# Shifted token mixing with eleven packed matmuls a block instead of twelve

## The chip, the cores and the metric

The kernel runs on one core of a Trainium2 chip. The metric is device time in microseconds; the time before is the median of three runs. TensorE does the matmuls, VectorE, ScalarE and GpSimd the arithmetic on rows, and SyncE issues the DMAs.

## The reference, cut to what matters

```python
xn  = _layernorm(x)                               # x: 2048 tokens x 448
out = x + irfft2(rfft2(xn) * W) + B(xn)

def B(x, w1, w2, w3, w4):
    h = _gelu(_layernorm(x) @ w1)                 # 448 x 448
    c = 112
    g0 = h[:, 0*c:1*c] shifted by +1 token        # zero at the ends
    g1 = h[:, 1*c:2*c] shifted by -1
    g2 = h[:, 2*c:3*c] shifted by +2
    g3 = h[:, 3*c:   ] shifted by -2
    x1 = x + concat(g0, g1, g2, g3) @ w2          # 448 x 448
    return x1 + _gelu(_layernorm(x1) @ w3) @ w4   # F = 1792
```

The change touches the line with `w2`: each output token takes four quarters of 112 channels from the tokens one and two before and after it.

## The kernel before, in words

**Tokens.** Token a*16 + b stands on partition a (0 to 127) in block b (0 to 15). A shift by one or two tokens is therefore a change of block, and at blocks 14, 15, 0 and 1 also a shift by one partition. The blocks are worked in four groups, `GRP` = 14, 15, 0, 1; then 2 to 5, 6 to 9, 10 to 13.

**Precision.** Each fp32 matrix product is done as three fp16 products: every operand is split in a high fp16 half and a fp16 remainder ("lo"), and hi x hi, hi x lo and lo x hi are summed in PSUM. `PASS` names these three.

**The stage in order.** 28 matmuls on zeros (`warm_up`) run while the first rows load. Normalised rows are transposed on TensorE (`T1`, for the first three groups) or by DMA (`turn`, for the last). `w1_in` makes the w1 product of a block, 11 matmuls: since 448 = 3 x 128 + 64, the two cross terms that have 64 rows share one matmul. `w1_unit` then applies the gelu in PSUM (ScalarE, L433), writes the hi half in fp16 (ScalarE, L434) and the lo half (VectorE, L435, one operation over 448 columns) into a buffer `hs_buf` of 2 x 4 quarters, each padded from 112 to 128 columns, and one DMA on SyncE's queue transposes that buffer (L438) into `hT[g]`, 8 tiles of 128 tokens. Group 0 has 16 zero columns ahead of each block, so that the shift over the partition edge is a slice that starts one column earlier or later.

`w2_tile(b)` (L442) then takes its four quarters from the transposed blocks b-1, b+1, b-2 and b+2, three passes each: 12 matmuls with 112 rows (L454). VectorE adds the result to the residual row (L456). `w2` arrives in one DMA on 112 partitions and is split into hi (ScalarE) and lo (GpSimd) in `w2p`.

Then comes `ln2`: the second layernorm, whose rows are split and transposed by DMA into `x2mem` (L490), and the channel MLP: `mlp_in` with w3 (L385), gelu, and the w4 product (L787). The Fourier part runs in the second half of the span beside the MLP.

**Memory.** `x2mem` holds, at different times, two of the five `hs_buf`, the raw w4 (four loads, L228) and the transposed `y` of the MLP. `w3raw` is loaded in parts; the last one (its t = 3) waits in the queue until the transposition of block 5 was issued.

**Order.** Engines run in program order as a scheduler has laid it out, by priority (`prio`) and by `behind(key)`, which keeps an operation behind others named in `after`. SyncE issues its DMAs in order too: one that waits holds up all that come later. In the stage its order before is: eight h transpositions as the units end, the w3raw rest, one h, four xT, two h between two y, the four w4 loads, two y, four h, `csm`.

Of the kernel before, what the change touches and what calls it, by code (L numbers as in the profile page):

```python
# [20 lines left out]
NB, NC = 16, 16  # L21
# [3 lines left out]
PASS = ((0, 0), (0, 1), (1, 0))  # L25
SHIFT = [1, -1, 2, -2]
WARM = 28
# [8 lines left out]
WMAX = [(1, 4), (1, 5), (1, 6), (2, 0), (2, 1), (2, 2), (2, 3), (2, 4)]  # L36
HS = 3
EVAC, FILL = 0, 100000
# [30 lines left out]
def constants():  # L69
# [20 lines left out]
    for c in range(NC):  # L90
        for j8, (k1, t) in enumerate(slots(c)):
            for j, (kr, s, base) in enumerate(rows(c)):
                if base != k1:
                    continue
                phi = tau * np.outer(np.arange(NB), kr + 128 * np.arange(16)) / S
# [28 lines left out]
def body(tc, nc, x, wf, w1, w2, w3, w4, c_g, c_n, c_small, out):  # L124
# [69 lines left out]
    def load_x(g):  # L194
        for b0 in sorted(GRP[g])[::2]:
            SY.dma_start(xt[b0 // 2], xv[:, b0:b0 + 2])

# [22 lines left out]
    load_w3([2])  # L220
    x2mem = pw.tile([128, 9 * F], F16, name="x2mem")
    x2all = x2mem[:, 0:8 * F].rearrange("p (j t n) -> p j t n", j=4, t=7)
    w4raw = x2mem.bitcast(F32)[:, F:].rearrange("p (f n) -> p f n", f=14)
    w4v = w4.rearrange("(f p) n -> p f n", p=128)
    W4F = (0, 4, 8, 11, 14)

    def load_w4(i):
        SY.dma_start(w4raw[:, W4F[i]:W4F[i + 1]], w4v[:, W4F[i]:W4F[i + 1]])  # L228

# [168 lines left out]
    def h_alloc(g):  # L398
        t = {0: 0, 1: 1, 2: 2, 3: 1}[g]
        hT[g] = pr.tile([128, 8, 512 if g else 592], F16, tag=f"h{t}", name=f"h{g}")  # L400
        if g == 0:
            P.memset(hT[g][:, :, 0:576].rearrange("p t (b a) -> p t b a", b=4)[:, :, :, 0:16], 0.0)
            P.memset(hT[g][:, :, 576:592], 0.0)

    def h_at(g, i):
        return 128 * i if g else 144 * i + 16

# [8 lines left out]

    hs_buf = [p1.tile([128, 2, 4, 128], F16, name=f"hs{i}") for i in range(HS)]
    for t in hs_buf:
        P.memset(t.rearrange("p i k n -> p (i k) n")[:, :, 112:], 0.0)

    for o in (0, 1024):
        hs_buf.append(x2mem[:, o:o + 1024].rearrange("p (i k n) -> p i k n", i=2, k=4))
        P.memset(hs_buf[-1].rearrange("p i k n -> p (i k) n")[:, :, 112:], 0.0)

    def w1_unit(g, i, pm=None):
        if pm is None:
            pm = bank(("tr" if g == 1 else "mm", "acc")[i // 2], f"pw1_{g}{i}")
            w1_in(g, [(i, pm)], range(4))
        c = CS[GRP[g][i]]
        pm = pm[:, :D]  # L430
        pv_ = pm.rearrange("p (k n) -> p k n", k=4)
        h = hs_buf[c % (HS if g == 3 else HS + 2)]
        A.activation(out=pm, in_=pm, func=AF.Gelu_apprx_tanh, scale=gsc[:, c:c + 1])  # L433
        u = A.activation(out=h[:, 0, :, 0:112], in_=pv_, func=AF.Copy, scale=h1)  # L434
        v = V.scalar_tensor_tensor(out=h[:, 1, :, 0:112], in0=pv_, scalar=h1, in1=h[:, 0, :, 0:112],  # L435
                                   op0=ALU.mult, op1=ALU.subtract)
        o = h_at(g, i)
        d = SY.dma_start_transpose(out=hT[g][:, :, o:o + 128], in_=h.rearrange("p i k n -> p (i k n)"))  # L438
        after[g, i] = u.ins, v.ins
        after["h", g, i] = (d.ins,)  # L440

    def w2_tile(b):  # L442
        pm = bank("sp", f"pw2_{b}")
        n = 0
        for k in (2, 0, 1, 3):
            src, o = b - SHIFT[k], 1
            if src < 0:
                src, o = src + NB, 0
            elif src >= NB:
                src, o = src - NB, 2  # L450
            g, i = WHERE[src]
            o += h_at(g, i) - 1
            for hi, wi in ((0, 0), (0, 1), (1, 0)):
                T.matmul(pm[:, :D], hT[g][:112, 4 * hi + k, o:o + 128], w2p[:, wi, k], start=n == 0, stop=n == 11)  # L454
                n += 1
        V.scalar_tensor_tensor(out=xb(b), in0=xb(b), scalar=cs[:, CS[b]:CS[b] + 1], in1=pm[:, :D],  # L456
                               op0=ALU.mult, op1=ALU.add)

    def ln2(bs, engines):
# [22 lines left out]
        for i in range(n):  # L482
            b, h, x_ = b0 + i, y[i // 2][:, i % 2], o[i // 2][:, i % 2]
            k = r[:, i:i + 1]
            u = A.activation(out=h[:, 0:D], in_=x_, func=AF.Copy, scale=k)
            V.scalar_tensor_tensor(out=h[:, 448:512], in0=x_[:, 384:448], scalar=k, in1=h[:, 384:448],
                                   op0=ALU.mult, op1=ALU.subtract)
            v = V.scalar_tensor_tensor(out=h[:, 512:896], in0=x_[:, 0:384], scalar=k, in1=h[:, 0:384],
                                       op0=ALU.mult, op1=ALU.subtract)
            d = SY.dma_start_transpose(out=x2all[:, b // 4][:, :, 128 * (b % 4):128 * (b % 4) + 128], in_=h)  # L490
            after[f"b{b0}"] = u.ins, v.ins, d.ins

    def unscale(p, part):
        t = part.rearrange("p (b n) -> p b n", b=2)
        SY.dma_start(t, xv[:, 2 * p:2 * p + 2])
        return lambda: V.scalar_tensor_tensor(out=xt[p], in0=xt[p], scalar=p12, in1=t, op0=ALU.mult, op1=ALU.add)

    def finish(b):
        t = xb(b)
        if b < 2:  # L500
            t = row()[:, :D]
            SY.dma_start(t, xv[:, b])
            V.scalar_tensor_tensor(out=t, in0=xb(b), scalar=p12, in1=t, op0=ALU.mult, op1=ALU.add)
        SY.dma_start(ov[:, b], t)

# [5 lines left out]
    def do_fold(b0):  # L511
        X = pfd.tile([128, 2, D + 1], F32, tag="xf", bufs=3, name=f"xf{b0}")
        after["X", b0] = (SY.dma_start(X[:, :, 0:D], xv[:, b0:b0 + 2]).ins,)
        with behind("f", *FOLD[b0 // 2]):
# [180 lines left out]
    def front(G, fp, tag):  # L695
        tok = slice(256 * (G % 2), 256 * (G % 2) + 256)
        pm = bank(tag, f"pw3_{G}{fp}")
        for ff in range(2):
            f = 2 * fp + ff
            mlp_in(pm[:, 256 * ff:256 * ff + 256], w3p, slice(128 * f, 128 * f + 128), x2all[:, G // 2], tok)  # L700
        with prio(EVAC):
# [65 lines left out]
    def back(G, fp):  # L767
# [10 lines left out]
        for i in range(2):  # L778
# [12 lines left out]
            if end:  # L791
                with prio(EVAC):
                    for r, to in parts:
                        V.scalar_tensor_tensor(out=xb(b)[:, r], in0=to, scalar=p34[:, min(G, 1):min(G, 1) + 1],  # L794
                                               in1=xb(b)[:, r], op0=ALU.mult, op1=ALU.add)
                        if G > 4:
                            SY.dma_start(ov[:, b, r], xb(b)[:, r])

# [50 lines left out]
    def w4_split(f):  # L849
        split_w(w4p[0][:, 0, f:f + 2], w4p[0][:, 1, f:f + 2], w4raw[:, f:f + 2], s4)  # L850

# [4 lines left out]
    with behind("n", 0):  # L856
        s1, r1 = powers(m1, 4, "1", "mm")
    h_alloc(0)
    first = [bank("mm" if k < 2 else "sp", f"pw1_0{k}") for k in range(4)]
# [12 lines left out]
    with behind("w1", 3):  # L872
        squares(m2[:112], flat(w2s[:112]))
    T1(1, range(3))
# [13 lines left out]
    with behind("a1"), behind("n", 2):  # L888
        for k in range(1, 4):
            w1_unit(0, k, first[k])  # L890
    with behind("na", 2):
        for k in range(4):
            split_w(w2p[:, 0, k], w2p[:, 1, k], w2s[:112, k], s2[:112], P)
    h_alloc(1)
    for k in range(4):
# [7 lines left out]
    with behind("a2"):  # L903
        n1 = [norm1(3, [P, P, P, P])]
    h_alloc(2)
    for k in range(4):
# [16 lines left out]
    for b in range(4, 8):  # L923
        w2_tile(b)
        with behind(*PIN[b - 4]):
            w3_split(2 * b - 8)
            w3_split(2 * b - 7)
            for i in (2 * b - 10, 2 * b - 9):
                if i >= 0:
                    squares(m4[:, i:i + 1], flat(w4raw[:, 2 * i:2 * i + 2]), junk4)  # L930
    squares(m4[:, 6:7], flat(w4raw[:, 12:14]), junk4)
    ln2([2, 3], [A, P])
    h_alloc(3)
    for k in range(4):
# [10 lines left out]
    for j in range(4):  # L945
        homes[j] = x2mem[:, F * j:F * j + F]
    w4t.update({j: m.rearrange("p (i k n) -> p i k n", i=2, k=4) for j, m in homes.items()})
# [121 lines left out]
```

## Time and profile before

| | |
|---|---|
| median of 3 runs | 410.78 us (410.74 to 410.94) |
| the profiled execution | 410.65 us |
| its span in the trace | 408.9 us |
| outside the span | 1.75 us |
| granted TensorE clock, mean | 1.0 |
| TensorE, VectorE, ScalarE, GpSimd busy | 98%, 81%, 63%, 23% of the span |
| the token-mixing product (L454) | 192 matmuls, 39.9 us, at 32.0 to 101.4 us |

A row of a timeline reads: start, length (us), engine, line, operation, output and input by their names in the program, tile sizes, count, and in brackets the idle time just ahead with what ended it. A group's row has count, busy time, mean of one in ns (matmuls overlap, so the mean is longer than the pitch), and idle time ahead. A row of the DMA view gives queue and operation, count, KB each, and the median time from issue to landing. In a DMA view of a window, the first row is the busy share of the 16 engines in 40 slices (9 is 90% or more), GB/s what was moved in each, and "packets" are the pieces.

### The profile page before, as it was taken

The page shows a single profiled execution, that of the slowest core. Times are in us where ns is not written, and L with a number is a line of the kernel's source. Part 1 is how long each engine was busy: PE and PEld are TensorE (multiplying, and loading weights), DVE is VectorE, ACT ScalarE, POOL GpSimd, SP SyncE. Part 2 cuts the span into 40 slices and gives each one's busy share as a digit, 9 for nine tenths or more (in the row PEclk, how much of TensorE's full clock was granted, in tenths as well). Part 3 has the DMA queues.
Part 4 walks back from the last instruction along what each step waited for, and adds up shares of the span by engine and source line. Part 5 has one row for each costly group of instructions (what it writes and reads, how often), then busy time and mean ns, then how long its engine had stood idle before and what let it go on. Part 6 is the DMA issues. An engine that isn't in the chain of part 4 may idle for free.

```text
span 408.9 us, 8745 instructions
## 1 busy us (share of the span) xinstructions
PE 402.3 (98%) x3409; PEld 299.0 (73%) x3409; DVE 330.7 (81%) x686; ACT 256.5 (63%) x434; POOL 95.3 (23%) x172
## 2 busy tenths in 40 slices
PE   7999999999999999999999999999999999999996
PEld 3655555765668777777887887877777779998995
DVE  4888999898857678887798888955899989966645
ACT  4698879973758866556598888863453554453431
POOL 3877720101336748400012111110000000000000
PEclk9999999999999999999999999999999999999999
DMA  8959879914786456516255666500011022100101
GB/s 278 354 192 179 153 149 321 177 62 90 156 231 202 137 196 210 170 59 183 63 145 143 155 156 171 147 27 3 24 68 69 25 88 85 55 2 2 45 2 45
DMA packets 56168, 51.28 MB, mean 125 GB/s; under 512 B 37632, under 2 KB 50496, under 8 KB 56128
## 3 DMA queue, kind: packets, MB, share of 16 engines
q1 hardware_dynamic: 56128, 50.74, 46.0%
q8 instruction: 26, 0.43, 0.4%
q14 instruction: 14, 0.11, 0.1%
HBM read 38.28 MB, written 3.67 MB: 103 GB/s over the span
## 4 chain that ended last, share of the span: by engine, by line
PE 94%; DVE 3%; DMA 2%; POOL 0%; issue 0%; ACT 0%; SPq 0%; POOLq 0%
PE pw L385 33%; PE acc L787 23%; PE pw L454 9%; PE pw L414 6%; PE side L757 4%; PE acc L757 3%; PE pu L646 3%; PE ps L543 3%; PE pe L667 2%; PE pp L601 2%; PE px L618 2%; PE py L688 2%; DVE sta L293 1%; DMA xt<-x 1%; DMA h<-hs 1%; PE pta L374 1%
## 5 line engine op out<-in xcount | busy, mean ns | idle before, releaser
L385 PE MATMUL pw<-x2mem,w3p 128*128 128x256 f16 x1232 | 151.1, 273 | 0.0
L385 PEld LDWEIGHTS <-w3p 128*128 128x128 f16 x1232 | 119.2, 98 | 20.6
L787 PE MATMUL acc<-w4p,hf 128*128 128x448 f16 (+1 forms) x516 | 105.4, 348 | 0.0
L787 PEld LDWEIGHTS <-hf 128*128 128x128 f16 x516 | 49.8, 98 | 36.5
L705 ACT ACTIVATE pw<-pw,pe 128x512 f32<-128x512 f32 x42 | 27.5, 655 | 35.7 <-PE pw L385 35.7
L708 DVE SCALAR_TENSOR_TENSOR hf<-pw,h,hf 128x512 f16<-128x512 f32 x42 | 31.3, 748 | 14.5 <-ACT hf L707 14.4
L454 PE MATMUL pw<-w2p,h 112*128 112x448 f16 x192 | 39.9, 352 | 0.8 <-DMA h<-hs 0.8
L414 PE MATMUL pw<-w1p,xT 128*128 128x448 f16 x176 | 35.4, 352 | 0.0
L627 POOL TENSOR_TENSOR z<-te 128x450 f32<-128x450 f32 x16 | 15.7, 982 | 70.3 <-DVE te L625 70.3
L454 PEld LDWEIGHTS <-h 112*128 112x128 f16 x192 | 18.6, 98 | 17.2 <-DMA h<-hs 1.0
L707 ACT ACTIVATE hf<-pw,h 128x512 f16<-128x512 f32 x42 | 28.7, 686 | 1.0
L414 PEld LDWEIGHTS <-xT 128*128 128x128 f16 x176 | 16.9, 98 | 16.4 <-DVE xT L379 0.8
L723 ACT ACTIVATE hz<-g,h 128x896 f16<-128x896 f32 x14 | 14.6, 1044 | 22.3 <-DVE g L720 22.2
L757 PEld LDWEIGHTS <-hz 128*128 128x128 f16 x294 | 28.2, 98 | 0.4
L608 ACT ACTIVATE pf<-pp 64x450 f16<-64x450 f32 x32 | 17.4, 544 | 12.3 <-DVE pf L609 8.0
L609 DVE TENSOR_TENSOR pf<-pp,pf 64x450 f16<-64x450 f32 x32 | 19.9, 622 | 3.4 <-ACT pf L608 3.0
L724 DVE SCALAR_TENSOR_TENSOR hz<-g,h,hz 128x896 f16<-128x896 f32 x14 | 16.1, 1150 | 7.6 <-ACT hz L723 7.6
L623 ACT ACTIVATE te<-px 64x450 f32<-64x450 f32 x32 | 17.3, 542 | 1.2 <-PE px L618 0.6
L526 POOL TENSOR_TENSOR f<-xr 128x452 f32<-128x452 f32 x16 | 16.4, 1046 | 0.6
L717 ACT ACTIVATE g<-pw,pe 128x512 f32<-128x512 f32 x14 | 9.6, 684 | 10.2 <-PE pw L385 10.1
L794 DVE SCALAR_TENSOR_TENSOR xt<-acc,p,xt 128x448 f32<-128x448 f32 (+1 forms) x17 | 10.9, 654 | 6.2 <-PE acc L787 6.0
L523 POOL TENSOR_TENSOR xr<-xf 128x452 f32<-128x452 f32 x8 | 9.7, 1211 | 26.7 <-issue 20.3
(183 smaller groups left out, 705.7 us busy)
## 6 DMA issues: line engine op xcount, KB each, us to landing
wc<-wf SPq DMA_DIRECT2D x32, 225.0 KB, 3.8
wl<-wf SPq DMA_DIRECT2D x8, 450.0 KB, 4.1
xt<-x SPq DMA_DIRECT2D x8, 448.0 KB, 7.9
xf<-x SPq DMA_DIRECT2D x8, 448.0 KB, 3.6
loads<-x SPq DMA_DIRECT2D x7, 448.0 KB, 4.0
out<-xt SPq DMA_DIRECT2D x13, 224.0 KB, 1.9
w3raw<-w SPq DMA_DIRECT2D x3, 896.0 KB, 12.6
gn<-c_g SPq DMA_DIRECT2D x16, 128.0 KB, 3.1
```

The lines of the kernel that those rows point to most:

```text
L385: T.matmul(ps_out, wp[:, wi + t, cols], xT[:, xi + t, tok], start=t == 0 and wi + xi == 0, stop=t == 3 and wi == 4)
L414: T.matmul(pm[:, :D], xTs[g][:, xi + t, 128 * i:128 * i + 128], w1p[:, wi + t], start=t == 0 and p == 0, stop=t == 3 and p == 2)
L454: T.matmul(pm[:, :D], hT[g][:112, 4 * hi + k, o:o + 128], w2p[:, wi, k], start=n == 0, stop=n == 11)
L526: P.tensor_tensor(out=f[:, :, k:k + 2].rearrange("p b s d -> p s b d"), in0=u[:, :, 0], in1=u[:, :, 1], op=op)
L608: A.activation(out=hi, in_=src, func=AF.Copy)
L609: V.tensor_tensor(out=lo, in0=src, in1=hi, op=ALU.subtract)
L623: A.activation(out=e[64 * h:64 * h + 64], in_=px_[64 - 64 * h:128 - 64 * h, :2 * DF], func=AF.Copy)
L705: A.activation(out=pm, in_=pm, func=AF.Gelu_apprx_tanh, scale=r3)
L707: i = A.activation(out=h[:, 0], in_=pm, func=AF.Copy, scale=h3)
L708: j = V.scalar_tensor_tensor(out=h[:, 1], in0=pm, scalar=h3, in1=h[:, 0], op0=ALU.mult, op1=ALU.subtract)
L757: m = T.matmul(to, h[:, hi, 128 * blk:128 * blk + 128], b[wi], start=new and n == 0, stop=n == 2 and (last if blk in (2, 5, 3, 0) else end ...
L787: m = T.matmul(to, h[:, hi, o:o + 128], w4p[0][:, wi, f, r], start=first and f % 2 == 0 and n == 0, stop=end and f % 2 == 1 and n == 2, sk ...
```

## The change

The h rows are written in the order in which the w2 product wants them, before they are transposed, so that the four quarters of a block stand side by side: 448 columns hi and 448 lo, 896 without padding, 7 tiles of 128 in place of 8 of 112 with padding. The product is then hi x hi and hi x lo for the first three tiles (6 matmuls), one for the last 64 rows of hi by the lo weights (the other 64 rows of that weight tile are zero), and four for tiles 3 to 6 by hi weights, where tile 3 holds the last 64 rows of hi and the first 64 of lo: 11 matmuls.

For this,

- blocks are renumbered by two (`at_token`), so that the partition edge lies between blocks 13 and 14;
- each unit writes its hi quarters in one operation and its lo quarters in two (two quarters each) into the rows (`slot`) of the four blocks that need them; rows live in `x2mem`, which grows from nine parts to ten;
- at the edge, four SBUF-to-SBUF DMAs on SyncE's queue (`wrap`, L430) move quarters by one partition, 127 rows each: two after the units of group 0, two after unit 13;
- a row is transposed once it is complete (`DONE`), 16 transpositions as before, of 7 tiles, into `hT` with two buffers of four blocks; the first four follow the units of group 0;
- `w2p` has 11 tiles of 128 rows; its hi half for the lo rows is shifted by 64 rows, which two more DMAs copy (229 and 172 KB, L904 and L905); `w2` loads in two DMAs on 128 partitions;
- w1's columns and w2's rows are permuted by quarters (`TURN`) on the way in;
- raw w4 goes partly into `x2mem` and partly into a buffer of its own; the order of the four loads differs, and so do the parts of `x2mem` that y uses.

In the stage SyncE's order is now: the two wraps of group 0, the two copies of w2p, four h transpositions, the w3raw rest, one h, three xT, y, one xT, one h, y, two h, the four w4 loads, one h, two y, three h, the two wraps of unit 13, four h, `csm`. From about 110 us on each engine has the same instructions in the same order as before.

```diff
-SHIFT = [1, -1, 2, -2]
+TURN = [3, 1, 0, 2]
+DONE = {c: [c - 2] for c in range(2, 12)} | {12: [10, 13], 13: [11, 12, 14, 15]}
+FIRST = 2
...
+    def at_token(b):
+        return (b + FIRST) % NB
...
-    SY.dma_start(w2s[:112], w2.rearrange("(k p) n -> p k n", p=112))
+    P.memset(w2s[64:128, 3], 0.0)
+    SY.dma_start(w2s[:, 0:3], w2[0:384].rearrange("(t p) n -> p t n", p=128))
+    SY.dma_start(w2s[0:64, 3], w2[384:448])
...
-    x2mem = pw.tile([128, 9 * F], F16, name="x2mem")
+    x2mem = pw.tile([128, 10 * F], F16, name="x2mem")
...
-    w2p = pr.tile([112, 2, 4, D], F16, name="w2p")
+    w2p = pr.tile([128, 11, D], F16, name="w2p")
...
+    def slot(b):
+        return x2mem[:, 896 * b + 3584:896 * b + 4480].rearrange("p (i n) -> p i n", i=2)
+
+    def slots_of(c, i):
+        t = slot(c - 2)[:, i]
+        return bass.AP(t.tensor, t.offset, [list(t.ap[0]), [3 * 896 + 224, 2], [896 + 112, 2], [1, 112]])
+
+    def wrap(to, own, by, k):
+        dst, src = slot(to)[:, :, k], slot(own)[:, :, k]
+        SY.dma_start(dst[1:128] if by else dst[0:127], src[0:127] if by else src[1:128])
...
-        u = A.activation(out=h[:, 0, :, 0:112], in_=pv_, func=AF.Copy, scale=h1)
-        v = V.scalar_tensor_tensor(out=h[:, 1, :, 0:112], in0=pv_, scalar=h1, in1=h[:, 0, :, 0:112],
-                                   op0=ALU.mult, op1=ALU.subtract)
-        o = h_at(g, i)
-        d = SY.dma_start_transpose(out=hT[g][:, :, o:o + 128], in_=h.rearrange("p i k n -> p (i k) n"))
+        u = A.activation(out=h[0], in_=pv_, func=AF.Copy, scale=h1)
+        for k in range(2):
+            v = V.scalar_tensor_tensor(out=h[1][:, k], in0=pv_[:, k], scalar=h1, in1=h[0][:, k],
+                                       op0=ALU.mult, op1=ALU.subtract)
+        if GRP[g][i] == 13:
+            wrap(-2, 14, 1, slice(224, 448))
+            wrap(-1, 15, 1, slice(336, 448))
+        for b in DONE.get(GRP[g][i], ()):
...
+            d = SY.dma_start_transpose(out=hT[b // 4][:, :, 128 * (b % 4):128 * (b % 4) + 128],
+                                       in_=slot(b if b < 14 else b - 16).rearrange("p i n -> p (i n)"))
...
-        for k in (2, 0, 1, 3):
...
-            for hi, wi in ((0, 0), (0, 1), (1, 0)):
-                T.matmul(pm[:, :D], hT[g][:112, 4 * hi + k, o:o + 128], w2p[:, wi, k], start=n == 0, stop=n == 11)
-                n += 1
+        h = hT[b // 4][:, :, 128 * (b % 4):128 * (b % 4) + 128]
+        for n, (k, w) in enumerate([(k, w) for k in range(3) for w in (k, k + 7)] + [(3, 10)] + [(k, k) for k in (3, 4, 5, 6)]):
+            T.matmul(pm[:, :D], h[:, k], w2p[:, w], start=n == 0, stop=n == 10)
...
+    wrap(12, -4, 0, slice(0, 112))
+    wrap(13, -3, 0, slice(0, 224))
...
+            r = slice(0, 128 if k < 3 else 64)
+            split_w(w2p[r, k], w2p[r, 7 + k], w2s[r, k], s2[r], P)
+        SY.dma_start(w2p[64:128, 3:7], w2p[0:64, 0:4])
+        SY.dma_start(w2p[0:64, 4:7], w2p[64:128, 0:3])
```

More of the change, by code (lines that the diff above doesn't have):

```diff
@@ L195, in load_x @@
         for b0 in sorted(GRP[g])[::2]:
-            SY.dma_start(xt[b0 // 2], xv[:, b0:b0 + 2])
+            SY.dma_start(xt[b0 // 2], xv[:, at_token(b0):at_token(b0) + 2])
     load_x(0)
@@ L220, in body, with w4raw @@
     load_w3([2])
-    x2mem = pw.tile([128, 9 * F], F16, name="x2mem")
-    x2all = x2mem[:, 0:8 * F].rearrange("p (j t n) -> p j t n", j=4, t=7)
-    w4raw = x2mem.bitcast(F32)[:, F:].rearrange("p (f n) -> p f n", f=14)
+    x2mem = pw.tile([128, 10 * F], F16, name="x2mem")
+    x2all = [x2mem[:, 2 * F * j:2 * F * j + 2 * F].rearrange("p (t n) -> p t n", t=7) for j in (1, 0, 2, 3)]
+    w4half = [x2mem.bitcast(F32)[:, 2 * F:2 * F + 4 * D].rearrange("p (f n) -> p f n", f=4),
+              p1.tile([128, 10, D], F32, name="w4half")]
     w4v = w4.rearrange("(f p) n -> p f n", p=128)
     W4F = (0, 4, 8, 11, 14)
+    def w4raw(f, n):
+        return w4half[f >= 4][:, f - 4 * (f >= 4):f - 4 * (f >= 4) + n]
     def load_w4(i):
-        SY.dma_start(w4raw[:, W4F[i]:W4F[i + 1]], w4v[:, W4F[i]:W4F[i + 1]])
+        f, n = W4F[i], W4F[i + 1] - W4F[i]
+        SY.dma_start(w4raw(f, n), w4v[:, f:f + n])
     csm = pc.tile([128, 2 * (256 + 2 * DF + 452 + 128)], F16, name="csm")
@@ L392, in body @@
     w1p = p1.tile([128, 8, D], F16, name="w1p")
-    w2p = pr.tile([112, 2, 4, D], F16, name="w2p")
+    w2p = pr.tile([128, 11, D], F16, name="w2p")
+    P.memset(w2p[64:128, 10], 0.0)
     hT = {}
[L398 to L406, printed above, removed]
     def w1_in(g, units, ts, passes=range(3)):
@@ L415, in w1_in @@
                                  start=t == 0 and p == 0, stop=t == 3 and p == 2)
[L417 to L423, printed above, removed]
+    def slot(b):
[6 more added lines that the diff above has]
+        SY.dma_start(dst[1:128] if by else dst[0:127], src[0:127] if by else src[1:128])
+    for b, by, k in ((-2, 1, slice(224, 448)), (-1, 1, slice(336, 448)), (12, 0, slice(0, 112)), (13, 0, slice(0, 224))):
+        P.memset(slot(b)[0:1, :, k] if by else slot(b)[96:128, :, k], 0.0)
     def w1_unit(g, i, pm=None):
@@ L430, in w1_unit @@
         pm = pm[:, :D]
-        pv_ = pm.rearrange("p (k n) -> p k n", k=4)
-        h = hs_buf[c % (HS if g == 3 else HS + 2)]
+        pv_ = pm.rearrange("p (i j n) -> p i j n", i=2, j=2)
+        h = [slots_of((GRP[g][i] + 2) % NB - 2, k) for k in range(2)]
         A.activation(out=pm, in_=pm, func=AF.Gelu_apprx_tanh, scale=gsc[:, c:c + 1])
-        u = A.activation(out=h[:, 0, :, 0:112], in_=pv_, func=AF.Copy, scale=h1)
-        v = V.scalar_tensor_tensor(out=h[:, 1, :, 0:112], in0=pv_, scalar=h1, in1=h[:, 0, :, 0:112],
-                                   op0=ALU.mult, op1=ALU.subtract)
@@ new lines, in w1_unit @@
+        if GRP[g][i] == 13:
+            wrap(-2, 14, 1, slice(224, 448))
+            wrap(-1, 15, 1, slice(336, 448))
+        for b in DONE.get(GRP[g][i], ()):
+            if b // 4 not in hT:
+                hT[b // 4] = pr.tile([128, 7, 512], F16, tag="h", bufs=2, name=f"h{b // 4}")
+            d = SY.dma_start_transpose(out=hT[b // 4][:, :, 128 * (b % 4):128 * (b % 4) + 128],
+                                       in_=slot(b if b < 14 else b - 16).rearrange("p i n -> p (i n)"))
+            after["h", g, i] = (d.ins,)
@@ L489, in ln2 @@
                                        op0=ALU.mult, op1=ALU.subtract)
-            d = SY.dma_start_transpose(out=x2all[:, b // 4][:, :, 128 * (b % 4):128 * (b % 4) + 128], in_=h)
+            d = SY.dma_start_transpose(out=x2all[b // 4][:, :, 128 * (b % 4):128 * (b % 4) + 128], in_=h)
             after[f"b{b0}"] = u.ins, v.ins, d.ins
@@ L512, in do_fold @@
         X = pfd.tile([128, 2, D + 1], F32, tag="xf", bufs=3, name=f"xf{b0}")
-        after["X", b0] = (SY.dma_start(X[:, :, 0:D], xv[:, b0:b0 + 2]).ins,)
+        after["X", b0] = (SY.dma_start(X[:, :, 0:D], xv[:, at_token(b0):at_token(b0) + 2]).ins,)
         with behind("f", *FOLD[b0 // 2]):
@@ L699, in front @@
             f = 2 * fp + ff
-            mlp_in(pm[:, 256 * ff:256 * ff + 256], w3p, slice(128 * f, 128 * f + 128), x2all[:, G // 2], tok)
+            mlp_in(pm[:, 256 * ff:256 * ff + 256], w3p, slice(128 * f, 128 * f + 128), x2all[G // 2], tok)
         with prio(EVAC):
@@ L872, in body @@
     with behind("w1", 3):
-        squares(m2[:112], flat(w2s[:112]))
+        squares(m2, flat(w2s))
     T1(1, range(3))
@@ L945, in body @@
     for j in range(4):
-        homes[j] = x2mem[:, F * j:F * j + F]
+        homes[j] = x2mem[:, F * (j ^ 2):F * (j ^ 2) + F]
     w4t.update({j: m.rearrange("p (i k n) -> p i k n", i=2, k=4) for j, m in homes.items()})
@@ L1053 @@
         "wf": np.stack([wr, wi], 2).transpose(0, 3, 2, 1, 4).reshape(NC, 64, 4 * DF).copy(),
-        "w1": np.ascontiguousarray(inputs["B_w1"]),
-        "w2": np.ascontiguousarray(inputs["B_w2"]),
+        "w1": np.concatenate([np.asarray(inputs["B_w1"])[:, 112 * k:112 * k + 112] for k in TURN], 1),
+        "w2": np.concatenate([np.asarray(inputs["B_w2"])[112 * k:112 * k + 112] for k in TURN], 0),
         "w3": np.ascontiguousarray(inputs["B_w3"]),
```

34 lines of the change are left out of this document (9 added, 25 removed).

## The prediction

> **What bounds the kernel now.** I read the page first (busy times, the chain that ended last, the costliest groups), then TensorE's waits, then the time from 28 to 86 us, where the changed stage runs.
>
> ```profile
> PE 402.3 (98%) x3409; PEld 299.0 (73%) x3409; DVE 330.7 (81%) x686; ACT 256.5 (63%) x434; POOL 95.3 (23%) x172
> PE 94%; DVE 3%; DMA 2%; POOL 0%; issue 0%; ACT 0%; SPq 0%; POOLq 0%
> L454 PE MATMUL pw<-w2p,h 112*128 112x448 f16 x192 | 39.9, 352 | 0.8 <-DMA h<-hs 0.8
> L414 PE MATMUL pw<-w1p,xT 128*128 128x448 f16 x176 | 35.4, 352 | 0.0
> ...
> PE wps L817 <- DVE wsrc L187: 1.2, 1, 1.2
> PE pm L249 <- DVE pt L247: 1.1, 1, 1.1
> PE pw L454 <- DMA h<-hs: 0.8, 1, 0.8
> ```
>
> TensorE is busy for 98% of the span and carries 94% of the chain. It waits three times, 3.1 us in all, and the last of these (0.8 us) is the token-mixing product's first wait for its transposed rows. After that TensorE never waits: whatever it no longer has to do comes off the end, and each new wait is added to it.
>
> The next two views are TensorE's timeline and the chain of waits (start, length, work).
>
> ```profile
> 1.22 7.53 PE L817 MATMUL wps<-wsrc 128*128 128x512 f16 x28 [1.22 <-DVE wsrc L187]
> ...
> 31.16 1.04 PE L374 MATMUL pta<-ident,xt 128*128 128x128 f32 x8
> ...
> 33.62 0.36 PE L454 MATMUL pw<-w2p,h 112*128 112x448 f16 x1 [0.79 <-DMA h<-hs]
> ...
> 47.10 8.51 PE pw L454 x45
> 84.90 2.27 PE pw L454 x12
> ```
>
> 45 matmuls of the product take 8.51 us on the chain and 12 take 2.27 us: 0.189 us each. Their 352 ns in the groups are pipelined, and are the same for a weight of 112 rows (L454) as for one of 128 (L414), so a fuller matmul costs no more than a padded one.
>
> **What the change removes.** A block takes 11 matmuls in place of 12. 16 x 0.189 = 3.0 us, all of it on a path where TensorE is the bound. This is the whole gain.
>
> **What it adds to VectorE and ScalarE.** The fp16 remainder of a unit, one operation of 448 columns, becomes two of 224.
>
> ```profile
> 29.62 1.27 DVE L435 SCALAR_TENSOR_TENSOR hs<-pw,h,hs 128x448 f16<-128x448 f32 x2
> ...
> 70.06 0.27 DVE L486 SCALAR_TENSOR_TENSOR y<-y,vs 128x64 f16<-128x64 f32 x1
> 70.25 0.61 DVE L488 SCALAR_TENSOR_TENSOR y<-y,vs 128x384 f16<-128x384 f32 x1
> ...
> 29.86 1.97 ACT L265 ACTIVATE w2p<-w2s 112x448 f16<-112x448 f32 x4
> ...
> sum 58.00, PE 57.21 PEld 33.66 DVE 53.76 ACT 50.13 POOL 20.56; mean PE 3.37 PEld 1.98 DVE 3.16 ACT 2.95 POOL 1.21
> ```
>
> Columns 64 and 384 differ by 0.34 us, 1.06 ns a column; 224 columns then take 0.27 + 160 x 0.00106 = 0.44 us as a lone record, about 0.36 when pipelined (two of 448 end in 1.27, so a record overlaps its neighbour by some 0.07). A pair is 0.72 against 0.60, so VectorE gains 16 x 0.12 = 2 us. The last row sums the busy times from 28 to 86 us: TensorE 57.2 goes to 54.2, VectorE 53.8 to 55.8. Off TensorE's path I count it at nothing, but the cover is thin (a rival below). ScalarE's operations keep their number.
>
> **What it adds to SyncE: order.** Before, a unit's rows are transposed as soon as the unit is done, block by block, and a product may begin with the quarters that have come. Now a row must be complete, and its first transposition stands in SyncE's queue behind two copies that shift rows by one partition (127 rows each, 224 and 448 bytes twice per row) and two copies of the weight's upper halves (229 and 172 KB).
>
> ```profile
> 28.20 4.77 SPq L438 DMA_TRANSPOSE h<-hs  x3
> ...
> 61.86 2.55 SPq L228 DMA_DIRECT2D x2mem<-w  x4
> 70.92 2.72 SPq L490 DMA_TRANSPOSE x2mem<-y  x2
> 73.74 6.62 SPq L438 DMA_TRANSPOSE h<-hs  x4
> 80.42 0.57 SPq L937 DMA_DIRECT2D csm<-c_small  x1
> ...
> h<-hs SPq DMA_TRANSPOSE x12, 3.2
> ```
>
> *First without the shift copies' own time.* The weight copies wait for ScalarE's last fp16 half, 29.86 + 1.97 = 31.8, and cost SyncE some 0.6 each (the csm row); so the first transposition is issued near 32.5 and lands 3.2 later, at 35.7, or 36.1 with part of 400 KB in front of it. TensorE has by then done 16 transpositions from 31.16 (1.04 for 8, so 1.9) and four matmuls of the next group (0.76): ready at 33.8. It waits 2.3 where it waited 0.8: +1.5. By the same counting the statistics product after the second block and the sixth block's product come some 0.5 and 0.3 late (their inputs all shift with SyncE's queue). The ninth block's transposition now stands right behind the four loads of w4:
>
> ```profile
> GB/s 156 210 205 159 215 206 197 159 218 209 82 76 115 229 378 382 378 363 378 378 387 440 378 373 392 382 401 397 401 387 382 385 373 373 302 257 203 46 29 19
> ...
> x2mem<-w SPq DMA_DIRECT2D x2, 896.0 KB, 6.7
> x2mem<-w SPq DMA_DIRECT2D x2, 672.0 KB, 10.0
> x2mem<-y SPq DMA_TRANSPOSE x1, 4.1
> ```
>
> (The first row is 59 to 74 us; the last the transposition issued at 70.92.) 3.1 MB at 380 GB/s are 8.3 us; two transpositions earlier in the queue, the loads start near 61 and the ninth block lands about 72.4. TensorE, 3.0 early and 2.3 late, comes to it near 71.8: +0.55. In sum 1.5 + 0.8 + 0.55 = 2.85 against 3.03 saved: the change would be nearly nothing.
>
> *Now the shift copies.* No copy in this trace has a row count like 127. Two windows give the price of a piece: 28 to 31 us holds transpositions of 256-byte pieces alone, 404 to 408.9 the last stores, about 1.07 KB a piece.
>
> ```profile
> DMA  0000000000000000000159999999999999998200
> DMA packets 1056, 0.26 MB, mean 87 GB/s; under 512 B 1056, under 2 KB 1056, under 8 KB 1056
> q1 hardware_dynamic: 1056, 0.26, 46.9%
> ...
> DMA packets 432, 0.46 MB, mean 94 GB/s; under 512 B 48, under 2 KB 432, under 8 KB 432
> q1 hardware_dynamic: 432, 0.46, 26.7%
> ```
>
> 46.9% of 16 engines for 3 us over 1056 pieces is 21.3 ns of one engine for 256 bytes; 26.7% of 16 x 4.9 us over 432 is 48.5 ns for 1.07 KB; on the line between them 20 ns for 224 bytes and 28 for 448. A shift copy has 127 x 2 = 254 pieces, so 5.1 us and 7.1 us of one engine, 12.2 for the pair; dealt over 16 engines it would be 0.8. The pieces of both windows, 1056 = 16 x 66 and 432 = 16 x 27, go evenly into 16, and the row counts behind them are multiples of 16. 127 is a prime: equal shares of whole rows exist only as one share of 127. If the chip deals in equal shares, as in both windows, the whole copy runs on one engine. I take that; on one engine the bounds for a pair are 9.5 (every piece at 18.6 ns, the 21.3 scaled by bytes to 224) and 17.4 (the second copy's pieces at 48.5); dealt over 16, it is the 0.8.
>
> [...]
>
> What is issued after a copy has its own share on that engine, behind it. First pair: issued from 28.3, first data some 1.2 after issue (slice 19 of the window's DMA row), 29.6 + 12.2 = 41.8; then the weight copies' share, 400 KB at 380 GB/s, 1.05; the first transposition's, 56 pieces x 21.3 ns = 1.2; landing 0.5 (3.2 less 1.2 of start and 66 x 21.3 ns of data): the first product starts at 44.6, not 36.1. **+8.5**. TensorE stands in its order meanwhile. The second pair is issued when unit 13 is done; before, that unit's transposition is the last of the four from 73.74 to 80.36, so about 79.7. The twelfth block's transposition stands behind the pair: 79.7 + 1.3 + 12.2 + 1.2 + 0.5 = 94.9, against TensorE's arrival near 85.1 (84.90 before, on the chain). **+9.8**. Both pauses stop TensorE for 10 us or so. At the start of the trace 28 matmuls of 512 columns took 7.53 us where 28 x 0.189 x 512/448 = 6.05 would do: coming out of idleness costs 1.5, so +3.0 for two; a pause of 1.1 us (the pm row of the waits) showed no such cost, hence the low bound 0 for it.
>
> [...]
>
> Sum: 410.65 (the profiled execution; its span is 408.9, and the median shown 410.78) - 3.03 + 2.85 + 8.5 + 9.8 + 3.0 = **431.8 us**. With the bounds of the pair (twice -2.7 or +5.2) and of the clock (-3.0): 423 to 442.
>
> **The rivals.**
> 1. *Copies dealt widely (cheap).* For it: nothing in the trace forces equal shares, every count here divided anyway. Then 410.65 - 3.03 + 2.85 + 2 x 0.1 = 410.7; if the ninth block isn't held by the w4 loads (-0.55) and the first transposition lands at 35.7 (-0.4), 409.7, faster. For their delay: a transposition behind loads took 4.1, not 3.0 to 3.2, at 70.92. Decides: whether the copies use more than four engines, i.e. end within 3 us.
> 2. *VectorE becomes the bound.* With cheap copies, 55.8 us of VectorE stand against 54.2 of TensorE. Should VectorE keep the 4.2 us of idle time that it has in the 58, the stage lasts 60.0 and the end is 412.7; against it, VectorE works ahead in that stage, and TensorE waits for it nowhere now.
> 3. *The packing isn't a saving*: were 128-row matmuls dearer than 112-row ones, 3.0 would not come; L414 against L454, 352 both, speaks against it, and I give it no chance of its own.
>
> **How the numbers follow.** A measurement of this kernel tells 0.2% (0.8 us) from no change. One engine per shift copy: 0.70, slower by all of its range. Cheap copies: 0.22, of which faster 0.09, same 0.10, slower 0.03. VectorE as the bound: 0.08, slower. So faster 0.09, same 0.10, slower 0.81. The likeliest case alone is 423 to 442. The range must reach toward the cheap case to leave out no more than 2 in 10: from 410.2 (below it lies half of the cheap case, 0.11) to 441 (above it 0.06).
>
> **What would show it.** Right: the product's line with 176 matmuls; the two early shift copies landing 5 to 13 us after issue; TensorE waiting 10 to 11 us for the first transposed block, and again near 10 us at the twelfth; a lower granted clock in slices right after. The statistics and the ninth block would wait under 1 us each. Wrong: shift copies that land within 3 us; or TensorE's long waits standing elsewhere (for VectorE's halves, for w4 or w3); or one pause only, were the second pair issued well before TensorE needs the twelfth block; or pauses without a lower clock.

## The result, and the profile after

The changed kernel takes 428.35 us (median of four runs, 428.21 to 429.25) against 410.81: a ratio of 1.0431 (95% interval 1.0413 to 1.0449). Its profiled execution has a span of 426.1 us, 17.2 more than before. The forecast was 431.8, its likeliest case 423 to 442.

The page of the changed kernel (busy times, granted clock in 40 slices of 10.7 us, the product's group) and TensorE's waits (us in total, times, longest):

```profile
PE 405.2 (95%) x3393; PEld 298.3 (70%) x3393; DVE 335.4 (79%) x702; ACT 255.6 (60%) x434; POOL 95.8 (22%) x171
PEclk9998899996999999999999999999999999999999
L463 PE MATMUL pw<-w2p,h 128*128 128x448 f16 x176 | 39.4, 379 | 12.4 <-DMA h<-x2mem 12.4
...
PE pw L463 <- DMA h<-x2mem: 12.4, 3, 6.1
PE pm L260 <- DVE pt L258: 1.9, 2, 1.4
PE wps L825 <- DVE wsrc L191: 1.2, 1, 1.2
PE ps L551 <- DVE y L556: 0.9, 1, 0.9
PE pta L385 <- DVE x2mem L446: 0.8, 1, 0.8
PE acc L795 <- ACT hf L715: 0.2, 1, 0.2
```

The 16 matmuls are gone (176), and TensorE's waits have grown from 3.1 to 17.4 us. 12.4 of them are three waits for a transposed block; TensorE's timeline says which:

```profile
42.01 4.03 PE L463 MATMUL pw<-w2p,h 128*128 128x448 f16 x11 [6.07 <-DMA h<-x2mem]
...
66.87 2.24 PE L463 MATMUL pw<-w2p,h 128*128 128x448 f16 x11
...
81.40 2.25 PE L463 MATMUL pw<-w2p,h 128*128 128x448 f16 x11 [1.89 <-DMA h<-x2mem]
...
98.88 4.29 PE L463 MATMUL pw<-w2p,h 128*128 128x448 f16 x11 [4.48 <-DMA h<-x2mem]
```

They are the first block (6.1 us), the ninth (1.9) and the twelfth (4.5). After the two long ones a block's 11 matmuls take 4.03 and 4.29 us in place of 2.24 (the row at 66.87 is the sixth block, at full clock). The windows (stretch, length, busy us of each engine with counts; then granted clock, DMA share, GB/s) show why: half clock.

```profile
42.00:45.00 3.00, 2.99 (x9) 1.22 (x10) 0.00 (x0) 0.00 (x0) 0.00 (x0) 0.50 1.14 203
46.00:52.00 6.00, 6.00 (x34) 3.10 (x32) 3.84 (x19) 0.76 (x2) 0.81 (x4) 1.00 0.47 101
98.80:102.80 4.00, 3.92 (x11) 1.65 (x12) 0.00 (x0) 0.00 (x0) 0.00 (x0) 0.50 1.02 124
```

The cause stands in the DMA view of two windows, 28 to 44 and 84 to 100 us (40 slices of 0.4 us), and in SyncE's timeline (start and length of each issue):

```profile
GB/s 0 0 0 0 2 36 17 17 17 17 17 17 17 20 7 16 21 21 21 21 21 21 21 196 208 313 226 99 195 148 27 16 143 285 289 282 291 179 207 218
w2p<-w2p SPq DMA_DIRECT2D x1, 224.0 KB, 4.5
w2p<-w2p SPq DMA_DIRECT2D x1, 168.0 KB, 8.3
...
GB/s 205 212 87 210 209 142 147 212 200 14 9 17 9 10 21 21 21 21 21 21 20 21 42 21 20 18 17 17 17 17 17 38 220 116 231 156 215 195 91 212
...
28.44 3.69 SPq L430 DMA_DIRECT2D x2mem<-x2mem  x2
32.23 4.38 SPq L905 DMA_DIRECT2D w2p<-w2p  x1
36.71 0.55 SPq L904 DMA_DIRECT2D w2p<-w2p  x1
37.35 5.68 SPq L455 DMA_TRANSPOSE h<-x2mem  x4
...
86.63 5.14 SPq L430 DMA_DIRECT2D x2mem<-x2mem  x2
92.21 8.65 SPq L455 DMA_TRANSPOSE h<-x2mem  x4
```

For 7 us the core moves 17 GB/s (224-byte pieces) and then 21 GB/s (448), where transpositions move over 200. That this is one engine at work, the trace shows piece by piece. Here is the DMA view of 0.1 us in the middle of the first copy (31.4 to 31.5 us, slices of 2.5 ns):

```profile
DMA  0040000400004000040000400004000040000040
DMA packets 8, 0.00 MB, mean 18 GB/s; under 512 B 8, under 2 KB 8, under 8 KB 8
```

Eight pieces start one behind the other, some 13 ns apart. Counted over the trace's DMA records, no more than two pieces of a shift copy ever overlap, the end of one with the start of the next; in e1 below, where most rows go in copies of 112, up to 17 and 21 do, the 448-byte pieces at up to 254 GB/s. The 254 pieces of 224 bytes run from 29.9 to 33.3 us and those of 448 from 33.3 to 39.6; the second pair takes 88.1 to 94.2 (448 bytes) and 94.2 to 97.5. A pair thus takes 9.7 and 9.4 us: 3.3 for the small pieces and 6.1 to 6.3 for the large ones, which follow each other 21 ns apart for most of the copy and more slowly for the rest: at its start (in the second from 88.1 to 89.8 us, while the core moved nothing else) and, in the first, beside other transfers from 38.4 us (448 B / 21 GB/s = 21 ns, 5.4 us for 254, is what they would take at that pace).

The first weight copy's issue (L905) then holds SyncE for 4.38 us where the second takes 0.55, and lands after 8.3 us; only at 37.35 is the first transposition issued.

### The profile page after: what moved, and what is told of

Its sections match the earlier page's. It is cut to its first block, busy times and chain, and to the rows that moved or that the text cites. A ratio compares the mean times of both kernels' runs of the same rounds, so it can differ in the third digit from the quotient of the medians.

```text
span 426.1 us, 8731 instructions
## 1 busy us (share of the span) xinstructions
PE 405.2 (95%) x3393; PEld 298.3 (70%) x3393; DVE 335.4 (79%) x702; ACT 255.6 (60%) x434; POOL 95.8 (22%) x171
## 4 chain that ended last, share of the span: by engine, by line
PE 63%; ACT 2%; POOL 1%; DVE 1%; issue 0%; POOLq 0%
PE pw L396 25%; PE acc L795 18%; PE side L765 4%; PE acc L765 3%; PE pu L654 3%; PE pe L675 2%; PE pp L609 2%; PE px L626 2%; PE py L696 2%; PE ps L551 2%; POOL f L534 1%; ACT xf L525 1%; ACT pw L713 0%; ACT xh L541 0%; DVE xh L542 0%
## 5 line engine op out<-in xcount | busy, mean ns | idle before, releaser
L463 PE MATMUL pw<-w2p,h 128*128 128x448 f16 x176 | 39.4, 379 | 12.4 <-DMA h<-x2mem 12.4
L713 ACT ACTIVATE pw<-pw,pe 128x512 f32<-128x512 f32 x42 | 27.5, 655 | 38.4 <-PE pw L396 38.3
L463 PEld LDWEIGHTS <-h 128*128 128x128 f16 x176 | 18.0, 104 | 30.7 <-DMA h<-x2mem 13.4
L616 ACT ACTIVATE pf<-pp 64x450 f16<-64x450 f32 x32 | 17.4, 543 | 12.3 <-DVE pf L617 8.0
L464 DVE SCALAR_TENSOR_TENSOR xt<-xt,cs,pw 128x448 f32<-128x448 f32 x16 | 10.8, 672 | 13.7 <-PE pw L463 13.7
L542 DVE TENSOR_TENSOR xh<-f,xh 128x452 f16<-128x452 f32 x16 | 12.9, 840 | 7.4 <-ACT xh L541 7.4
L534 POOL TENSOR_TENSOR f<-xr 128x452 f32<-128x452 f32 x16 | 17.5, 1115 | 0.6
L443 ACT ACTIVATE pw<-pw,gsc 128x448 f32<-128x448 f32 x16 | 9.2, 596 | 13.9 <-issue 13.9
```

The source lines that it names most:

```text
L463: T.matmul(pm[:, :D], h[:, k], w2p[:, w], start=n == 0, stop=n == 10)
L534: P.tensor_tensor(out=f[:, :, k:k + 2].rearrange("p b s d -> p s b d"), in0=u[:, :, 0], in1=u[:, :, 1], op=op)
L616: A.activation(out=hi, in_=src, func=AF.Copy)
```

## The experiments

Medians, with ratios to the kernel before measured beside them (410.8 to 411.1 us). "Without" means that the part is left out of the computation, as each expectation says.

**Split copies (e1).** Each shift copy becomes 112 + 15 rows; the order of all else stays until about 90 us, where a few matmuls and two loads change places.

```diff
-        SY.dma_start(dst[1:128] if by else dst[0:127], src[0:127] if by else src[1:128])
+        d, s = (dst[1:128], src[0:127]) if by else (dst[0:127], src[1:128])
+        SY.dma_start(d[0:112], s[0:112])
+        SY.dma_start(d[112:127], s[112:127])
```

> Each shift copy of 127 rows issued as two, of 112 and 15 rows; the order of everything else is kept. Theory (one engine: rows are dealt in equal shares, so 127 rows go to one engine, and what is issued later waits behind its share): the data of a pair takes under 1 us in place of 9.7 and 9.4, the first product waits some 1.6 us in place of 6.1 (the added copies cost SyncE 1.4 us), the wait at the twelfth block and the half clock go: 413 to 415 us. Rival (small pieces inside SBUF are dear by themselves): the same number of pieces, so 427 to 429. Rival (complete rows in a fixed order are what costs): 425 to 428.

Measured: 415.59 us, ratio 1.0115 (1.0099 to 1.0132). The DMA view of 28 to 34 us (landing in us), TensorE's timeline, and the DMA view of 66 to 74 us:

```profile
x2mem<-x2mem SPq DMA_DIRECT2D x1, 98.0 KB, 2.2
x2mem<-x2mem SPq DMA_DIRECT2D x1, 49.0 KB, 2.2
x2mem<-x2mem SPq DMA_DIRECT2D x1, 6.6 KB, 2.1
x2mem<-x2mem SPq DMA_DIRECT2D x1, 13.1 KB, 2.1
...
37.70 3.80 PE L465 MATMUL pw<-w2p,h 128*128 128x448 f16 x11 [2.07 <-DMA h<-x2mem]
...
77.41 2.26 PE L465 MATMUL pw<-w2p,h 128*128 128x448 f16 x11 [2.31 <-DMA h<-x2mem]
...
w4half<-w SPq DMA_DIRECT2D x1, 672.0 KB, 10.7
h<-x2mem SPq DMA_TRANSPOSE x1, 10.7
```

The same bytes in twice as many DMAs each land in 2.2 us. 12.8 us of the loss go by this edit alone, and the wait at the twelfth block with them. This bears out one engine, and speaks against small pieces and against the fixed order as the main cause, the two rivals named ahead of the run. But 4.8 us stay, a little over the expected 413 to 415. The first block waits 2.07 us, and its matmuls still run at half clock for the most part (3.80 us where 2.24 would do; the granted clock is 0.64 on average from 37.0 to 41.5 us); the ninth waits 2.31: its transposition lands together with the w4 load in front of it, 10.7 us after issue.

**Row counts (e3).** 126, 125, 121 and 112 rows in place of 127.

```diff
+        n = {12: 126, 13: 125, -2: 121, -1: 112}[to]
+        SY.dma_start(dst[1:1 + n] if by else dst[0:n], src[0:n] if by else src[1:1 + n])
```

> The four copies with 126, 125, 121 and 112 rows in place of 127 (1 to 15 rows of each are left out). [...] If a copy merely stops being cheap when 16 doesn't divide it: the first three take 3 to 6 us each, 420 to 427. Small pieces: 1 to 12% fewer pieces, 425 to 428.

Measured: 417.69 us in a single run. The first row is the DMA view of 28 to 34 us (slices of 0.15 us), the second of 82 to 88:

```profile
GB/s 0 0 0 0 0 0 0 0 0 0 0 0 16 157 139 119 0 0 0 0 0 0 0 0 0 0 0 0 0 0 0 42 81 87 96 111 245 269 278 200
...
GB/s 195 53 32 183 218 218 210 215 208 198 50 0 0 0 96 146 161 194 120 48 166 108 74 0 0 0 68 210 225 217 174 217 224 147 34 14 84 203 213 215
```

With 126 rows the first copy moves up to 157 GB/s and is done in 0.5 us, against 17 GB/s and 3.3 us with 127: one row fewer, a seventh of the time. With 125 (slice 33 on) the rate is 81 to 96 until the weight copies join, 4 to 5 times the 21 of one engine, and up to 8 pieces overlap; 121 rows (slices 15 to 20 of the second row) run at up to 194 and 112 (the next three) at up to 166. With 126, 121 and 112 rows up to 16 or 17 pieces overlap. So 127 rows (one engine) and 125 stand apart from the other three, which the rates don't tell from one another. The forecast's equal shares of whole rows fit that: 127 is a prime, and five shares of 25 rows come near the 4 to 5 times measured. How many engines each of the other three used is not shown; that 16 doesn't divide 126 or 121 did not make them dear. The time lies below both ranges given, and 2.1 us over e1's: the waits that e1 has are here too (2.25 us at the first block, with 3.94 us for its 11 matmuls after it, and 1.92 at the ninth), and 1.4 us of waits behind the stage that e1 has not.

**No copies (e2).**

```diff
-        SY.dma_start(dst[1:128] if by else dst[0:127], src[0:127] if by else src[1:128])
+        pass
```

> The four shift copies are left out (the quarters that cross a partition edge stay zero). One engine: as with split copies less their 1.4 us and more of SyncE, 412 to 414 us, with the price of complete rows alone left in it. Small pieces: also 412 to 414. Complete rows: 424 to 427, since the order is unchanged.

Measured: 415.11 us in a single run: over the expected range, and no better than split copies. So some 4 us of the loss belong to the rest of the change. That split copies cost nothing does not follow: at the first block this kernel does better than e1 (a wait of 0.91 us in place of 2.07, and full clock behind it: 0.999 is granted in the mean of the run, 0.996 in e1), but SyncE's order is another too. With no copy to wait for, `csm` and the transpositions of two edge blocks go into the queue earlier, and TensorE waits 1.5 us behind the stage where e1 does not. Only the sums are alike.

**Moved copies (e4).** 127 rows, but later in SyncE's queue.

```diff
-        if GRP[g][i] == 13:
-            wrap(-2, 14, 1, slice(224, 448))
-            wrap(-1, 15, 1, slice(336, 448))
...
-    wrap(12, -4, 0, slice(0, 112))
-    wrap(13, -3, 0, slice(0, 224))
...
         load_w3([3])
+        wrap(12, -4, 0, slice(0, 112))
+        wrap(13, -3, 0, slice(0, 224))
...
         for b in DONE.get(GRP[g][i], ()):
+            if b == 14:
+                wrap(-2, 14, 1, slice(224, 448))
+                wrap(-1, 15, 1, slice(336, 448))
```

> The copies keep 127 rows, but the first pair is issued behind the first four transpositions and the last part of w3, the second behind the transpositions of the twelfth and thirteenth block. One engine, and the queue behind it is what costs: the copies still take 9 to 10 us a pair, but only transpositions needed 10 us later stand behind them; no wait over 2 us at the first and the twelfth block, 411 to 416 us. If the copies disturb whatever runs beside them, wherever they stand: 420 to 428. Complete rows: 425 to 428.

Measured: 418.37 us, ratio 1.0194 (1.0174 to 1.0213). SyncE's timeline and TensorE's waits:

```profile
40.18 6.47 SPq L430 DMA_DIRECT2D x2mem<-x2mem  x2
47.27 4.98 SPq L455 DMA_TRANSPOSE h<-x2mem  x1
...
PE pw L463 <- DMA h<-x2mem: 3.8, 3, 2.2
PE pw L463 <- DVE mvb L305: 2.9, 1, 2.9
```

The long waits at the first and twelfth block are gone though the copies are as slow as ever: what costs is the queue behind them. But the cover was too short: the fifth block's transposition, the next one behind the pair, is held at issue for 4.98 us (1.3 is usual), a new wait of 2.2 us follows, and another (2.9) at the ninth block. The time is 2.4 us over the expected range.

**One copy in the kernel before (e5, e6).** A copy that nobody reads, of 127 or 112 rows, behind the fourth transposition.

```diff
+    with behind("h", 0, 3):
+        SY.dma_start(dmy[0:127, 0:2, 0:224], dmy[1:128, 2:4, 0:224])    # e6: 0:112, 16:128
```

> The kernel before, with one copy of 127 rows x 2 x 448 bytes between unused columns added behind the fourth transposition; nobody reads what it writes. One engine: its 254 pieces at 21 to 25 ns hold one engine from about 34 to 40 us; the fifth transposition, which lands near 36.5 before, lands near 41, and the products that wait for it and the matmuls behind them stand 3 to 5 us: 414 to 417 us. Rival (only complete rows in a fixed order make such a copy dear): 410.8 to 411.8.

> The same copy with 112 rows. One engine: 112 rows go to 16 engines, data under 1 us and 0.7 us of SyncE: 410.8 to 411.8 us. Rival (small pieces are dear by themselves): 12% fewer pieces than with 127 rows, so the same time within 0.5 us as that kernel, if that one is slower.

Measured: 423.27 us (1.0312, 1.0288 to 1.0335) and 416.45 us (1.0135, 1.0120 to 1.0151). They are 6.3 and 4.7 us over what was expected, and part of it is a matter of order: with one DMA more, the scheduler laid out the following stage anew (the first y transposition comes at 69.7 us in e6, not at 56.5), so neither compares cleanly with the kernel before. With each other they do, since all five engines have the same order in both: 15 rows more cost 6.8 us. TensorE's timeline of e5 and the DMA view of 35 to 45 us of e5, then of e6:

```profile
43.71 2.42 PE L456 MATMUL pw<-w2p,h 112*128 112x448 f16 x6 [4.78 <-DMA h<-x2mem]
...
h<-x2mem SPq DMA_TRANSPOSE x1, 8.1
...
x2mem<-x2mem SPq DMA_DIRECT2D x1, 98.0 KB, 2.9
```

The transposition behind the 127-row copy lands after 8.1 us, TensorE stands 4.8 us, and its clock is halved afterwards (6 matmuls in 2.42 us; 0.50 granted from 43.7 to 46.0 us). In e6 that wait is absent, and the copy lands in 2.9 us. Small pieces by themselves are out: in e6 the 224 pieces pass in 0.8 us (35.8 to 36.6), in e5 the 254 take 6.2 (36.1 to 42.2).

**w4 behind the ninth block (e7).** On e1: two of the four loads of w4 issued behind that transposition.

```diff
-        for i in range(4):
+        for i in (1, 2):
             load_w4(i)
...
     for k in range(4):
         w1_unit(3, k)
+        if k == 0:
+            with behind("h", 3, 0):
+                load_w4(0)
+                load_w4(3)
```

> Split copies, and the third and fourth load of w4 issued behind the ninth block's transposition (and the squares that read them moved along). If the ninth block waits because 3.1 MB of w4 stand in front of it: with 1.6 MB the wait of 2.3 us goes, 412.8 to 414 us. If it waits for its unit and not for the queue: the wait stays, 415 to 416.5.

Measured: 414.33 us, ratio 1.0070 (1.0047 to 1.0093). Its five runs fall into two kinds by their granted clock: 1.0 and 412.67 us twice, 0.995 to 0.996 and 414.33 to 415.09. The profiled execution is one of the first kind; the ninth block no longer waits in it. TensorE's waits and its timeline:

```profile
PE pw L465 <- DMA h<-x2mem: 3.1, 2, 2.0
...
37.76 2.25 PE L465 MATMUL pw<-w2p,h 128*128 128x448 f16 x11 [2.03 <-DMA h<-x2mem]
```

The longest (2.0) is the first block's, as in e1, but here the full clock holds after it: 2.25 us for the same 11 matmuls. The other wait (1.1) is at 88 us, later than any of e1's. So the queue in front did cause the ninth block's wait. 1.3 of its 2.3 us arrive in the median. After the same pause of 2 us the clock was lost in e1's trace and kept in this one; that the slower runs here lost it at this pause is likely by their mean clock (e1's is 0.996 too), but none of them was traced.

**First block first (e8).** On e1: the first transposition ahead of the weight copies, and the shift copies where e4 has them.

```diff
     for k in range(4):
         w1_unit(1, k)
+        if k == 0:
+            with behind("h", 1, 0):
+                SY.dma_start(w2p[64:128, 3:7], w2p[0:64, 0:4])
+                SY.dma_start(w2p[0:64, 4:7], w2p[64:128, 0:3])
```

> Split copies, with the first block's transposition issued ahead of the two copies of w2 and all shift copies behind the first four transpositions and the last part of w3, the second pair behind the transpositions of the twelfth and thirteenth block. If the first wait (2.2 us) and the half clock after it (1.5) come from what stands ahead of that transposition: 411.5 to 413 us, with the ninth block's wait left. If complete rows alone make it late: 415 to 416.5.

Measured: 412.20 us, ratio 1.0036 (1.0020 to 1.0052). TensorE's and VectorE's timelines:

```profile
36.04 1.31 PE L465 MATMUL pw<-w2p,h 128*128 128x448 f16 x6 [1.04 <-DMA h<-x2mem]
...
31.02 3.30 DVE L448 SCALAR_TENSOR_TENSOR x2mem<-pw,h,x2mem 128x224 f16<-128x224 f32 x9
```

As expected: the first product starts at 36.0 (42.0 in the changed kernel), after a wait of 1.0 us, with its clock whole (1.00 from 30 to 120 us). VectorE's halves take 3.30 us for nine, some 0.36 each, the price that the forecast had. The ninth block still waits, 1.1 us: its transposition lands 10.2 us after issue, as in e1.

**Both (e9), and two more tries.** e9 has the edits of e7 and e8. e10 also takes the units of group 0 from behind the third group's statistics. e11 is e9 without the shift copies.

```diff
-    with behind("a1"), behind("n", 2):
+    with behind("a1"):                      # e10
         for k in range(1, 4):
             w1_unit(0, k, first[k])
```

> The two last edits together (first block's transposition ahead of the copies, shift copies split and later, two of the w4 loads behind the ninth block's transposition). If the waits that they take away are separate: 412.2 less the ninth block's 1.2 us, so 410.5 to 411.5 us, no change against the kernel before. If the 3.0 us of matmuls were to be had in full: 408 to 409. If the waits only move on: 412 to 413.

> As the combined kernel, but the units of group 0 no longer stand behind the third group's statistics on VectorE, so that their lo halves are written some 2 us earlier and the first block's row is complete earlier; the third group's normalisation comes later by as much. If the rest of the loss is the first block's late row (pauses of 0.8, 0.2 and 1.2 us around 33 to 36 us): 409.5 to 411 us. If the normalisation is then what is late: 412 to 414.

> The combined kernel without the four shift copies (the quarters that cross a partition edge stay zero). If the copies, split and moved, cost nothing any more: the same as the combined kernel within 0.7 us, 411.5 to 413.5. If they still hold something up: 409 to 411.

Measured: e9 412.77 us (1.0045, 1.0029 to 1.0060), e10 423.13 (1.0287, 1.0270 to 1.0304), e11 416.73 (1.0136, 1.0118 to 1.0153). e9 falls in the range of the case in which the waits only move on; e10 and e11 lie over all that was expected of them. The waits of e9 with the product (or w4's), then those of e10, then SyncE and TensorE of e11:

```profile
PE pw L465 <- DMA h<-x2mem: 1.6, 2, 1.0
PE acc L797 <- ACT hf L717: 0.4, 1, 0.4
PE acc L797 <- DVE hf L718: 0.4, 1, 0.4
...
PE pw L396 <- DMA x2mem<-y: 5.0, 1, 5.0
PE pta L385 <- POOL xt L334: 3.1, 1, 3.1
...
76.12 0.57 SPq L954 DMA_DIRECT2D csm<-c_small  x1
76.79 6.15 SPq L455 DMA_TRANSPOSE h<-x2mem  x4
...
82.12 5.82 PE L463 MATMUL pw<-w2p,h 128*128 128x448 f16 x22 [4.11 <-DMA h<-x2mem]
```

In e9 the ninth block's wait is gone against e8, but the time isn't lower: the waits moved on, and even its best run, 411.64, is above the kernel before. In e10 the normalisation is late instead (3.1 us), and the stage behind it is laid out anew, with y 5.0 us late. In e11 the two edge blocks can be transposed early, which lets the 643 KB of `csm` into the queue ahead of four transpositions that are needed sooner, and TensorE waits 4.1 us for one of them. It has no shift copy at all and is slower than e9 with them, so it can't price the copies; that `csm` alone makes the wait was not tested. No version measured here beats the kernel before; the nearest, e8, is 0.36% behind it.

## Why the prediction was right or wrong

**Forecast and sign: right, for the reason given.** Each shift copy of 127 rows ran on one engine, 9.7 and 9.4 us a pair; what stood behind it waited. e1, e3 and the pair e5/e6 show it, each with another edit, and the pieces in the trace, which run one behind the other. That equal shares are the cause is the forecast's inference, which e3's 125 rows support.

**The gain, 3.0 us: right in size.** At full clock a block's 11 matmuls take 2.24 us (the row at 66.87), of which 0.16 is the end of the last: 0.189 each, as before, for 176 in place of 192. The waits take the gain, and more.

**The price of a pair, 12.2 us: too high.** The pairs took 9.7 and 9.4 us, at the low bound of 9.5. The step that failed is reading 20 and 28 ns a piece from windows in which all 16 engines worked: the one engine took 13 ns for the small pieces and 24 to 25 on average for the large ones (21 for most of the copy).

**First pause, 10.8 us of waiting: 6.1 measured.** The product starts at 42.0, not 44.6, by the pair that was 2.5 us cheaper; and TensorE came to it at 35.9 rather than 33.8, having begun its transpositions 0.5 us later, waited 0.8 for VectorE (a lo half, L446) and taken some 0.8 longer over them and the four matmuls.

**Second pause, +9.8 us: 4.5 measured.** The pair was issued at 86.6 where 79.7 had been taken, and TensorE came at 94.4 where 85.1 had been taken. The forecast let the first pause add in full to a second one reckoned on the old clock; but the stall had held TensorE 9.3 us and SyncE only 6.9, so 2.4 us of the second pause were used up; the cheaper pair takes 2.8 more, and 9.8 less both is 4.6.

**Half clock, +3.0: 3.8 measured** (4.03 + 4.29 less twice 2.25, so 1.8 and 2.0 where the forecast had 1.5 each), and 0.4 more on the w3 matmuls behind the second (13 take 1.94 us, 1.59 before). Right in kind and place, a little low.

**Order without the copies, 2.85 us: too low.** e1 prices that case at 415.6, not 410.7, so the first rival was mis-sized by 5 us, and its "faster" end was never near. The ninth block waited 2.3 us there and not 0.55 (1.9 in the changed kernel, where the prediction's signs had under 1). The forecast had the length right, 11.4 us from the loads' first data to the block's landing, but in e1 that data begins at 66.0 and not near 61, and TensorE comes to the block at 75.1 and not at 71.8. The first block's wait of 2 us was followed by half clock, 1.6 us that the rival had not. Without any shift copy (e2) the first transposition is issued at 33.5 and not at 32.5, which leaves room for only one of the two weight copies at 0.6 us each. The statistics product was 0.5 late, as forecast; the sixth block's wait did not come.

**What the forecast had not**: 1.1 us of waits in the tail (the ps and acc rows), though from 137 us on TensorE's order is the same as before; and a late start. TensorE's first transpositions (the pta rows) begin at 10.8 us in the changed kernel and at 10.4 to 11.0 in the versions made from it, against 10.3 before. Why isn't shown.

**VectorE as the bound** did not come: 0.36 us a half, and no large wait for it, though TensorE waited 0.8 us for one of its lo halves.

So the sum was near (431.8 against 428.35) partly by luck, because of opposite errors: pauses and half clock were taken at 21.3 us where e1 regains 12.8, 8.5 too much, and the rest was some 5 too low.

What stays open: why SyncE's issue is held. It is not the one-engine copies alone: in the changed kernel a transposition behind the four w4 loads is held too, for 4.41 us (at 71.13). And how much of e9's last 1.9 us is the row that must be complete and how much the new layout of the stage or the late start (0.5 us in e9): they change together in every edit here.

## What to carry to other kernels

Look at the row count of every copy before its bytes: 127 rows took some seven times as long as 126 or 112 here, because one engine did the work, and a copy split into 112 + 15 rows landed in 2.2 us. A DMA that was off the path still held what was issued after it on that queue (4.98 us at issue in e4, 1.3 otherwise); so order a queue by when each landing is needed. And before trading matmuls for a layout, count the waits that the old layout avoided: here every version of the new layout lost more in all than the 3 us of TensorE that it saved.

## What the runs showed of the hardware that was not expected

- One engine moved a 224-byte piece inside SBUF every 13 ns and a 448-byte piece every 21 ns for most of a copy (24 to 25 on average over it); the estimate from shared windows was 20 and 28.
- Behind copies on one engine the issuing engine itself was held: the next DMA took 4.38 us to issue behind a pair (a weight copy, 0.55 otherwise), 4.98 behind a pair in e4 and 5.61 behind a single copy in e5 (a transposition each, 1.3 otherwise).
- A pause of 2.0 us could already cost half the clock: 11 matmuls took 3.80 us after 2.07 (e1) and 2.25 after 2.03 (e7). From 37.0 to 41.5 us the granted clock is 0.64 on average in e1 and 1.00 in e7. If e1's half clock lasts to the end of that stretch, it begins at 38.3 us, half a us after the pause (an estimate from these figures). What decides whether such a pause costs the clock is not shown.
- Not of the chip but of the scheduler: with one more DMA that nothing depends on, the following stage was laid out in another order, and the kernel was 5.4 us slower (e6).
